# The last steps of a decode layer: inverse roots by one power instruction, the residual's product ahead, a store of two rows

## The chip, the cores and the metric

The kernel runs on one core of a Trainium2 chip. The metric is the device time of one execution in microseconds (us), and the number compared is the median of several runs.

## The reference

One token (one row of 512 numbers) passes two blocks:

```
h   = x + A(layernorm(x))
out = h + B(layernorm(h))

A: q = x @ wq                      (512 -> 32 heads of 128)
   8 key/value heads, 16384 cached positions, 4 query heads to each
   softmax(q . k / sqrt(128)) @ v, then @ wo   (4096 -> 512)
B: one position, so the four shifted quarters of its mixer are all zero:
   x1 = x;  B = x1 + gelu(layernorm(x1) @ w3) @ w4   (512 -> 1792 -> 512)
layernorm(x) = (x - mean) / sqrt(var + 1e-5)
```

Block B gets a normalised row and normalises it again, so two inverse roots of nearly the same variance are needed at the end: `1/sqrt(v + eps)` for the residual and one of `v (1 + eps) + eps^2` for what goes into GELU. The output is `hr + (hr - mean) * root + gelu(...) @ w4`, where `hr` is the row h.

## The kernel before, in words

The work is written out by hand. A small `Program` class collects instructions for each engine in the order in which they are written, and derives the semaphore waits from the tiles that each reads and writes; `_run` issues an engine's instructions one after another. Nothing reorders them. `dve(None)` and `pe(None)` mark a branch that is never taken otherwise; what is written behind the mark lies in another block of code.

The stages are these. (1) The row's statistics: `row_sums(0, ...)` and `variance(0)` give mean and variance on all 128 partitions, `seeds` and `inverse_root` the root, and line 577 the normalised row `xn`. GpSimd (POOL) clears `qb` and `pt` meanwhile. (2) The query: 32 products with wq (L586). (3) Four passes over pairs of key/value heads: keys are loaded in 4 MB halves, transposed by VectorE (L609), multiplied (L626), softmax (L636 to L651), values multiplied (L662), gathered. (4) The output product with wo (L728), `osum`, `row_sums(1, ...)`, `hc`, 16 products with w3 (L746). (5) The tail: roots, GELU in two halves (L758), each transposed to `hcol` (L762), 14 chunks `m` of 4 products each with w4 (L772), the copy `fin` (L777), the store (L778).

All large loads are issued on SP's queue (helper `load`, L433) in the order in which they are written: wq, keys and values, then wo, w3 and w4 in pieces. w4 comes in four pieces, `W4 = ((0, 5), (5, 10), (10, 13), (13, 14))`, and the products of chunk m wait for the piece that holds m.

The inverse root before is an integer seed and three Newton steps:

```
    by(lambda e: e.tensor_scalar(vh, v, -0.5, None, ALU.mult), ...)
    for k in range(3):
        by(lambda e: e.tensor_scalar(z, y, y, vh, ALU.mult, ALU.mult), ...)
        by(lambda e, dst=dst: (...)(dst, z, 1.5, y, ALU.add, ALU.mult), ...)
```

At the end VectorE works out the root for GELU and GpSimd the other one at the same time; GpSimd goes on with `xs` and `xsum` (L753, L755). `xsum`, the residual, is added by a product with the identity matrix into the accumulator of the w4 products (L768), behind chunk 9. The accumulator `n_ps` has 128 rows: the 32 rows of quarter o all hold the same 128 outputs, and the store takes one row of each quarter.

## Time and profile before

| | us |
|---|---|
| median of 3 runs | 191.78 |
| the runs | 191.37 to 191.93 |
| span of the profiled execution, first to last instruction | 190.4 |
| time of the profiled execution outside its span | not given |

| engine | busy us | share of the span |
|---|---|---|
| TensorE (PE) | 118.6 | 62% |
| VectorE (DVE) | 118.2 | 62% |
| ScalarE (ACT) | 9.3 | 5% |
| GpSimd (POOL) | 7.3 | 4% |

The DMA engines moved 79.20 MB at a mean of 416 GB/s. In the rows of the profile, a time in front is the start in us from the first instruction of the program, the next number is the length; x32 is a count; what stands behind <- in square brackets is what ended the engine's idle time before the row. A row of the windows has the stretch, its length, the busy time of each engine with its count, the granted TensorE clock (1.00 is full), the share of the DMA engines and GB/s.

### The profile page before, as it was taken

To read this page: it belongs to the slowest core of one execution; us is meant where nothing else is said; L and a number is where in the kernel's file an instruction comes from. 1 tells how busy PE (TensorE), PEld (TensorE's weight loads), DVE (VectorE), ACT (ScalarE), POOL (GpSimd) and SP (SyncE) were. 2 spreads that over 40 slices of the span, in tenths; PEclk is the share of its full clock that TensorE was granted. 3 is DMA by queue.
4 is the path that set the end of the run, shared out by engine and by line. 5 is a ranking of instruction groups with operands and counts; after the bars stand their busy time and mean duration, and the time that the engine had idled before them with its cause. 6 is when DMAs were issued, how large, how long until landed. Compare 5 with 4: busy or idle time off the path is not lost.

```text
span 190.4 us, 2182 instructions
## 1 busy us (share of the span) xinstructions
PE 118.6 (62%) x695; PEld 46.1 (24%) x695; DVE 118.2 (62%) x155; ACT 9.3 (5%) x16; POOL 7.3 (4%) x16
## 2 busy tenths in 40 slices
PE   0119709996195599940944989508449995294644
PEld 0103203442031143310311433203113332031212
DVE  6740799995504989845049989350479895504370
ACT  3000000000200000011000000020000000500020
POOL 7100000000000000000000000000000000000060
PEclk9999985899958579995585899975979999758855
DMA  6999999999999999997999999979999999989991
GB/s 227 434 441 441 441 441 441 441 441 441 413 441 406 420 523 441 441 441 330 441 441 441 523 441 413 441 324 420 413 441 441 441 441 441 441 367 421 409 411 51
DMA packets 3619, 79.20 MB, mean 416 GB/s; under 512 B 416, under 2 KB 544, under 8 KB 1568
## 3 DMA queue, kind: packets, MB, share of 16 engines
q1 hardware_dynamic: 3608, 79.17, 97.2%
q8 instruction: 1, 0.02, 0.0%
q14 instruction: 2, 0.02, 0.0%
q10 hardware_dynamic: 8, 0.00, 0.0%
HBM read 79.17 MB, written 0.00 MB: 416 GB/s over the span
## 4 chain that ended last, share of the span: by engine, by line
PE 39%; DMA 37%; DVE 16%; issue 4%; ACT 2%; ACTq 0%; SPq 0%; DVEq 0%
DMA kb<-in_A_k_cache_dram 31%; PE banks L626 22%; PE banks L662 6%; DMA vb<-in_A_wq_dram 6%; DVE kt L609 6%; PE banks L586 5%; DVE pt L651 3%; PE banks L728 2%; DVE mx L636 1%; ACT p_sb L647 1%; PE banks L620 1%; DVE od L681 1%; PE banks L772 1%; DVE qcol L593 1%; PE banks L639 1%
## 5 line engine op out<-in xcount | busy, mean ns | idle before, releaser
L609 DVE STREAM_TRANSPOSE kt<-kb 128x2048 int32<-128x2048 int32 (+1 forms) x37 | 71.3, 1987 | 4.3 <-DMA kb<-in_A_k_cache_dram 2.8
L626 PE MATMUL banks<-kt,qn 128*128 x256 | 68.7, 414 | 0.5
L626 PEld LDWEIGHTS banks<-kt,qn 128*128 x256 | 26.2, 102 | 41.4 <-issue 24.6
L662 PE MATMUL banks<-vb,pt 128*32 128x512 bf16 x256 | 24.4, 565 | 2.8 <-POOLq L448 2.8
L678 DVE TENSOR_SCALAR od<-banks,rowc 128x128 f32<-128x128 f32 x4 | 1.4, 350 | 26.3 <-PE banks L662 26.3
L620 PE MATMUL banks<-qn 128*128 128x512 bf16 x8 | 4.0, 495 | 17.3 <-DVE kt L609 17.1
L651 DVE STREAM_TRANSPOSE pt<-p_sb 64x1024 bf16<-64x1024 bf16 x8 | 9.9, 1239 | 5.4 <-ACT p_sb L647 5.3
L662 PEld LDWEIGHTS banks<-vb,pt 128*32 128x32 bf16 x256 | 9.0, 136 | 16.4 <-issue 12.4
L586 PE MATMUL banks<-vb,xn 128*128 x32 | 8.9, 446 | 6.1 <-DVE xn L577 6.1
L669 PE MATMUL banks<-acc,zd 128*32 128x1 f32 x8 | 1.1, 202 | 17.7 <-DVE pt L651 17.7
L647 ACT ACTIVATE p_sb<-banks,bias 128x1024 bf16<-128x1024 f32 x4 | 4.5, 1113 | 155.4 <-DVE nmh L643 155.4
L636 DVE TENSOR_REDUCE mx<-banks 128x1 f32<-128x1024 f32 x4 | 4.9, 1224 | 8.1 <-PE banks L626 8.1
L593 DVE STREAM_TRANSPOSE qcol<-banks 64x1024 f32<-64x1024 f32 x4 | 4.8, 1226 | 6.9 <-PE banks L586 6.9
L528 POOL TENSOR_SCALAR st<-st 128x1 f32<-128x1 f32 x1 | 0.2, 241 | 176.1 <-DVE st L513 176.1
L586 PEld LDWEIGHTS banks<-vb,xn 128*128 128x128 bf16 x32 | 3.6, 112 | 11.0 <-issue 8.5
L639 PE MATMUL banks<-mxd,mean 128*128 128x128 f32 x8 | 2.0, 326 | 6.6 <-DVE mxd L637 6.6
L620 PEld LDWEIGHTS banks<-qn 128*128 128x128 bf16 x8 | 0.8, 100 | 20.2 <-issue 20.0
L684 PE MATMUL banks<-od,zo 128*32 128x128 f32 x8 | 1.6, 285 | 6.5 <-DVE od L681 6.5
L669 PEld LDWEIGHTS banks<-acc,zd 128*32 128x32 f32 x8 | 0.7, 140 | 18.4 <-DVE pt L651 18.4
L681 DVE SCALAR_TENSOR_TENSOR od<-banks,rowc,od 128x128 f32<-128x128 f32 x12 | 4.2, 351 | 0.4
L550 DVE CAST ident<-ident_f 4x4 bf16<-4x4 f32 x1 | 3.8, 3848 | 0.6 <-POOL ident_f L545 0.6
L728 PE MATMUL banks<-kb,o_b 128*32 128x512 bf16 x32 | 3.5, 583 | 1.1 <-DVE o_b L724 1.1
(78 smaller groups left out, 44.6 us busy)
## 6 DMA issues: line engine op xcount, KB each, us to landing
kb<-in_A_k_cache_dram SPq DMA_DIRECT2D x8, 4096.0 KB, 29.7
vb<-in_A_v_cache_dram SPq DMA_DIRECT2D x2, 4096.0 KB, 29.2
vb<-in_A_wq_dram SPq DMA_DIRECT2D x1, 4096.0 KB, 12.3
kb<-in_A_wo_dram SPq DMA_DIRECT2D x2, 1536.0 KB, 25.4
kb<-in_B_w_dram SPq DMA_DIRECT2D x2, 640.0 KB, 25.4
kb<-in_B_w_dram SPq DMA_DIRECT2D x1, 896.0 KB, 22.4
kb<-in_B_w_dram SPq DMA_DIRECT2D x2, 448.0 KB, 23.4
kb<-in_A_wo_dram SPq DMA_DIRECT2D x1, 768.0 KB, 28.5
```

Source lines behind the costliest of these rows:

```text
L586: pe(lambda e, k=k: e.matmul(row[:, bass.ds(P.b, 512)], copies(xn[:, k:k + 1], 128), wq_k[:, k, bass.ds(P.c, REP * DH)], start=(k == 0), s ...
L593: dve(lambda e, g=g, b=b, half=half: e.transpose(qcol[64 * g:64 * g + 64, 2 * b:2 * b + 2, :, :].rearrange("p e m u -> p (e m u)"), half.r ...
L609: P.op("DVE", lambda e, view=view: e.transpose(view(kt), view(kb[y])), r=[("r", y, i) for i in range(RPARTS)], w=[("kt", t + i) for i in r ...
L620: pe(lambda e: e.matmul(row[:, bass.ds(P.y, 512)], copies(none, 128), copies(none, 512), start=True, stop=False, skip_group_check=True), r ...
L626: pe(lambda e, n=n: e.matmul(row[:, bass.ds(P.y, 512)], qn[:, n, bass.ds(P.q, 128)], key_piece(P.k, n), start=False, stop=(n == 3), skip_g ...
L636: dve(lambda e: e.tensor_reduce(mx[:, :], s_all, AX.X, ALU.max), r=[("s", 0), ("s", 1)], w=["mx"], **both)
L639: pe(lambda e: e.matmul(m_ps[:, 0:128], mean4[:, :], mxd[:, :], start=True, stop=True), r=["mxd", "mean4"], w=["m"], bank=["mn"])
L647: act(lambda e: e.activation(p_sb[:, :], s_all, ACTF.Exp, bias=bias[:, 0:1], scale=float(SCALE), accum_out=acc[:, :]), r=[("s", 0), ("s", ...
L651: dve(lambda e, g=g: e.transpose(pt[64 * g:64 * g + 64, :, :, g, :], p_sb[64 * g:64 * g + 64, :]), r=["p"], w=["pt"])
L662: pe(lambda e, l=l, ct=ct, ch=ch: e.matmul(O_ps[0][32 * ct:32 * ct + 32, :], pt[:, l, ch, :, :].rearrange("p g u -> p (g u)"), tiles[:, l ...
L681: dve(lambda e, block=block, c=c: e.scalar_tensor_tensor(od[:, :], block, rowc[:, c:c + 1], od[:, :], ALU.mult, ALU.add), r=[key, "rowc", ...
L728: pe(lambda e, r_=r_, q=q: e.matmul(O_ps[0][32 * q:32 * q + 32, :], copies(o_b[:, r_:r_ + 1], 32), wo_sb[:, r_ * D:(r_ + 1) * D], start=(r ...
```

## The change

Three things are done in the tail, and one in both places where a root is needed.

The roots: `seeds` and `inverse_root` go; a tile `expo` of two columns is filled with -0.5 by GpSimd, and one GpSimd `tensor_tensor` with the operation `pow` gives the root, of one column in the first layer norm and of two columns at once in the last. In the first, this instruction stands in GpSimd's order ahead of the two clearing instructions for `qb` and `pt`. `xs` and `xsum` are worked out by VectorE, ahead of the two transposes to `hcol`, and only the second needs the root.

The residual's product stands behind chunk 6 instead of chunk 9, and is made in four products of 32 columns.

The quarters of the accumulator are filled in the order 0, 2, 1, 3 (`BLOCK`). ScalarE copies the lower 64 rows to the left half of `fin`, VectorE the upper 64 rows to the right half, and the store takes rows 31 and 32 of `fin`, two rows of 256 numbers (512 bytes), where before it took four rows of 128 (256 bytes). VectorE's copy is behind the mark `dve(None)`.

```diff
+BLOCK = (0, 2, 1, 3)
...
-        def seeds(i, ns):
...
-        def inverse_root(i, n, by):
...
+            for n in range(1 + i):
                 mul, add = (1.0 + EPS, EPS * EPS) if n else (1.0, EPS)
                 dve(lambda e, n=n, mul=mul, add=add: e.tensor_scalar(s[:, 4 + n:5 + n], s[:, 3:4], mul, add,
                                                                      ALU.mult, ALU.add), r=[(S, 3)], w=[(S, 4 + n)])
...
+            pool(lambda e: e.tensor_tensor(s[:, 6:7 + i], s[:, 4:5 + i], expo[:, 0:1 + i], ALU.pow),
+                 r=["expo"] + [(S, 4 + n) for n in range(1 + i)], w=[(S, 6 + n) for n in range(1 + i)])
...
+        pool(lambda e: e.memset(expo[:, :], -0.5), w=["expo"])
...
         variance(0)
-        seeds(0, (0,))
-        inverse_root(0, 0, dve)
         act(lambda e: e.activation(scr[0:1, 0:1], mean4[0:1, 0:1], ACTF.Exp), r=["mean4"], w=["scr"])
         pool(lambda e: e.memset(qb[:, :, :, :], 0.0), w=["qb"])
         pool(lambda e: e.memset(pt[:, :, :, :, :], 0.0), w=["pt"])
...
         variance(1)
-        seeds(1, (0, 1))
-        inverse_root(1, 1, dve)
-        inverse_root(1, 0, pool)
-        pool(lambda e: e.tensor_scalar(xs[:, :], hr[:, :], s[:, 0:1], s[:, 6:7], ALU.add, ALU.mult),
-            r=["hr", (S, 0), (S, 6)], w=["xs"])
-        pool(lambda e: e.tensor_tensor(xsum[:, :], hr[:, :], xs[:, :], ALU.add), r=["hr", "xs"], w=["xsum"])
+        dve(lambda e: e.tensor_scalar(xs[:, :], hr[:, :], s[:, 0:1], None, ALU.add), r=["hr", (S, 0)], w=["xs"])
+        dve(lambda e: e.scalar_tensor_tensor(xsum[:, :], xs[:, :], s[:, 6:7], hr[:, :], ALU.mult, ALU.add),
+            r=["hr", "xs", (S, 6)], w=["xsum"])
...
         for m in range(NHC):
+            if m == NHC // 2:
+                for o in range(4):
+                    pe(lambda e, o=o: e.matmul(
+                        n_ps[32 * o:32 * o + 32, 0:128], ident_f[:, 32 * BLOCK[o]:32 * BLOCK[o] + 32], xsum[:, :],
+                        start=False, stop=False, skip_group_check=True),
+                       r=["ident_f", "xsum"], w=["n"], bank=["mn"])
             if m == W4[-2][0]:
-                pe(lambda e: e.matmul(n_ps[:, 0:128], ident_f[:, :], xsum[:, :], start=False, stop=False,
-                                      skip_group_check=True), r=["ident_f", "xsum"], w=["n"], bank=["mn"])
                 pe(None)
             for o in range(4):
                 pe(lambda e, m=m, o=o: e.matmul(
-                    n_ps[32 * o:32 * o + 32, 0:128], hcol[:, m, :], w4_sb[:, m, o * 128:(o + 1) * 128],
+                    n_ps[32 * o:32 * o + 32, 0:128], hcol[:, m, :], w4_sb[:, m, BLOCK[o] * 128:(BLOCK[o] + 1) * 128],
...
-        act(lambda e: e.activation(fin[:, :], n_ps[:, 0:128], ACTF.Identity), r=["n"], w=["fin"], bank=["mn"])
-        P.op("SP", lambda e: e.dma_start(out[0, 0:1, :].rearrange("o (q j) -> (o q) j", q=4), fin[0:128:32, :]),
-             r=["fin"], w=["out"], dma="out")
+        act(lambda e: e.activation(fin[:, 0:128], n_ps[0:64, 0:128], ACTF.Identity),
+            r=["n"], w=[("fin", 0)], bank=["mn"])
+        dve(lambda e: e.tensor_copy(fin[:, 128:256], n_ps[64:128, 0:128]), r=["n"], w=[("fin", 1)], bank=["mn"])
+        P.op("SP", lambda e: e.dma_start(out[0, 0:1, :].rearrange("o (q j) -> (o q) j", q=2), fin[31:33, :]),
+             r=[("fin", 0), ("fin", 1)], w=["out"], dma="out")
```

More of the change, by code (lines that the diff above doesn't have):

```diff
@@ L386, in bass_sequential_preLN__gqa_block_cached__mixer_s_mlp__decode_kernel @@
         st = [sb(f"st{i}", [128, 16], FP32) for i in range(2)]
-        sti = [sb(f"sti{i}", [128, 4], I32) for i in range(2)]
+        expo = sb("expo", [128, 2], FP32)
         xn = sb("xn", [128, NCH], BF16)
@@ L414, in bass_sequential_preLN__gqa_block_cached__mixer_s_mlp__decode_kernel @@
         hcol = sb("hcol", [128, NHC, 32], BF16)
-        fin = sb("fin", [128, 128], BF16)
+        fin = sb("fin", [64, 256], BF16)
         kb_all = sb("kb", [128, 256 * DH], BF16)
@@ L503, in variance @@
                 r=[(S, 2)], w=[(S, 3)])
-        def seeds(i, ns):
-            s, t = st[i], sti[i]
-            S, T = ("st", i), ("sti", i)
-            lo, hi = min(ns), max(ns) + 1
-            for n in ns:
+            for n in range(1 + i):
                 mul, add = (1.0 + EPS, EPS * EPS) if n else (1.0, EPS)
@@ L514, in seeds @@
                                                                      ALU.mult, ALU.add), r=[(S, 3)], w=[(S, 4 + n)])
-            dve(lambda e: e.tensor_single_scalar(t[:, 2 + lo:2 + hi], s[:, 4 + lo:4 + hi].bitcast(I32), 1,
-                                                 ALU.arith_shift_right),
-                r=[(S, 4 + n) for n in ns], w=[(T, 2)])
-            dve(lambda e: e.tensor_scalar(t[:, lo:hi], t[:, 2 + lo:2 + hi], -1, 1597463007,
-                                          ALU.mult, ALU.add), r=[(T, 2)], w=[(T, n) for n in ns])
-        def inverse_root(i, n, by):
-            s, t = st[i], sti[i]
-            S, T = ("st", i), ("sti", i)
-            v, y = s[:, 4 + n:5 + n], t[:, n:n + 1].bitcast(FP32)
-            z = s[:, 8 + n:9 + n]
-            vh = s[:, 10 + n:11 + n]
-            by(lambda e: e.tensor_scalar(vh, v, -0.5, None, ALU.mult), r=[(S, 4 + n)], w=[(S, 10 + n)])
-            for k in range(3):
-                dst, key = (s[:, 6 + n:7 + n], (S, 6 + n)) if k == 2 else (y, (T, n))
-                by(lambda e: e.tensor_scalar(z, y, y, vh, ALU.mult, ALU.mult),
-                   r=[(T, n), (S, 10 + n)], w=[(S, 8 + n)])
-                by(lambda e, dst=dst: (e.scalar_tensor_tensor if by is dve else e.tensor_scalar)(
-                    dst, z, 1.5, y, ALU.add, ALU.mult),
-                   r=[(S, 8 + n), (T, n)], w=[key])
+            pool(lambda e: e.tensor_tensor(s[:, 6:7 + i], s[:, 4:5 + i], expo[:, 0:1 + i], ALU.pow),
+                 r=["expo"] + [(S, 4 + n) for n in range(1 + i)], w=[(S, 6 + n) for n in range(1 + i)])
         load("x4", x4[:, :], A_x[0, 0:1, :].rearrange("o (q j) -> (o q) j", q=4), "x4", "ACT")
```

## The prediction

> **What bounds the kernel now.** I read the page first (its span and the 40 slices), then the chain that ended last, then the timeline of the last 12 us, and last the issue and landing of the last weight pieces.

> ```profile
> span 190.4 us, 2182 instructions
> DMA  6999999999999999997999999979999999989991
> GB/s 227 434 441 441 441 441 441 441 441 441 413 441 406 420 523 441 441 441 330 441 441 441 523 441 413 441 324 420 413 441 441 441 441 441 441 367 421 409 411 51
> ```

> A slice is 4.76 us. The 16 DMA engines are busy from the first slice to the last but one, near 441 GB/s: the kernel is the time to read its weights and caches, and after that a tail. What lies under the stream can be shortened without any effect on the end. So I need the moment at which the stream's last pieces land. The last three pieces of w4 are these, first their issue (start, length) and then their size and the time from issue to landing:

> ```profile
> 159.74 5.84 SPq L433 DMA_DIRECT2D kb<-in_B_w_dram  x1
> 165.63 3.16 SPq L433 DMA_DIRECT2D kb<-in_B_w_dram  x1
> 168.83 0.43 SPq L433 DMA_DIRECT2D kb<-in_B_w_dram  x1
> ...
> kb<-in_B_w_dram SPq DMA_DIRECT2D x1, 640.0 KB, 26.0
> kb<-in_B_w_dram SPq DMA_DIRECT2D x1, 384.0 KB, 21.1
> kb<-in_B_w_dram SPq DMA_DIRECT2D x1, 128.0 KB, 18.2
> ```

> Second piece (m = 5 to 9): 159.74 + 26.0 = 185.74. Third (m = 10 to 12): 165.63 + 21.1 = 186.73. Fourth (m = 13): 168.83 + 18.2 = 187.03. Against that stands the end of the chain:

> ```profile
> 80.21 29.02 DMA kb<-in_A_k_cache_dram
> ...
> 183.61 0.20 DVE st L533
> ...
> 183.89 0.49 ACT hg L758
> ...
> 184.41 0.59 DVE hcol L762
> ...
> 185.04 1.45 PE banks L772 x36
> 186.49 0.73 PE banks L768 x2
> 187.21 0.58 PE banks L772 x10
> ...
> 187.81 0.28 ACT fin L777
> ```

> The chain view draws a line from the root (L533) through GELU (L758), transpose (L762) and last product (L772) to the end. It hides that the weights were a second wait of nearly the same size:

> ```profile
> 185.76 0.46 PEld L772 LDWEIGHTS banks<-kb,hcol 128*32 128x32 bf16 x20 [0.26 <-DMA kb<-in_B_w_dram]
> 186.41 0.50 PEld L768 LDWEIGHTS banks<-xsum,ident_f 128*128 128x128 f32 x2 [0.20 <-issue]
> 187.14 0.62 PE L772 MATMUL banks<-kb,hcol 128*32 128x128 bf16 x16
> ```

> At 185.76, 0.02 after the second piece, TensorE resumed after a DMA wait. From there it never stopped until 187.76: twenty products, the residual's product (L768, 186.41 to 187.14), then the sixteen that need pieces three and four. When those sixteen began at 187.14, both pieces had landed, the last 0.11 before. So the residual's product, and not the stream, set the last 0.4 us of TensorE. Behind it stands a fixed tail: copy, store, landing.

> **The change part by part.** The sum is made on this profiled execution (span 190.4; its own time outside the span is not given), and the difference is put on the median of the runs, 191.78, which is 1.38 above the span.

> *Residual's product.* It becomes four products of 32 columns (8 passes in place of 2) behind m = 6 instead of m = 9. Since m = 5 and 6 need the second piece, it still runs after 185.74; it does not fall into the wait ahead of that. Its price at 32 columns is seen at one place, L734, the same shapes:

> ```profile
> 179.32 0.43 PE L734 MATMUL banks<-osum,row 128*32 128x128 f32 x8 [0.79 <-DVE osum L732]
> 179.30:179.47 0.17, 0.15 (x8) 0.16 (x8) 1.00 0.70 274
> 186.41:187.14 0.73, 0.73 (x6) 0.50 0.14 41
> ```

> L734 took 0.43 with its drain, but at a granted clock of 1.00 (the third number from the end); at 186.4 the clock is 0.50. A round of four L772 products costs 0.10: the sixteen took 0.62, which is three steps of 0.10 and 0.32 for the last round with its drain. The residual costs between 0.11 (0.43 less that drain, if the clock cost nothing) and 0.73 (as now); I take 0.5, nearest to the L734 row slowed by the clock. Then, from 185.76: two rounds, 185.96; residual, 186.46; three rounds for m = 7 to 9, 186.77; the third piece is there since 186.73, so three rounds, 187.08; the fourth piece since 187.03, last round 0.32, end at 187.40. Before, 187.76: **-0.36**. Bounds: with a residual of 0.11 the landing at 187.03 plus 0.04 plus 0.32 stops it at 187.39; with 0.73 it is 187.63, -0.13.

> *Both roots by one GpSimd instruction.* Gone are two DVE integer steps and seven DVE steps of the Newton root for GELU (181.80 to 183.81), and seven steps and two wide ones on GpSimd. Added: one power of 128x2 on GpSimd, and two 128x128 steps on DVE ahead of the transposes.

> ```profile
> 181.56 0.21 DVE L513 TENSOR_SCALAR st<-st 128x1 f32<-128x1 f32 x2
> 181.57 1.68 PE L746 MATMUL banks<-kb,hc 128*32 128x448 bf16 x16 [0.69 <-ACT hc L740]
> 181.80 0.24 POOL L528 TENSOR_SCALAR st<-st 128x1 f32<-128x1 f32 x1 [176.12 <-DVE st L513]
> 185.22 0.45 POOL L755 TENSOR_TENSOR xsum<-hr,xs 128x128 f32<-128x128 f32 x1
> ```

> The inputs are ready at 181.77, so the power starts about 181.83. No row shows a power. Its bounds are the GpSimd step of one element, 0.24, and the longest GpSimd span of the trace, 2.18 (L560, below); it is nearest to a TENSOR_TENSOR, 0.45, with more arithmetic, and I take 0.8. GELU could then start at 182.7, but the product L746 that it reads ends at 183.25: the wait moves there. GELU at 183.3 instead of 183.89, transposed 1.1 later, first L772 at about 184.45 instead of 185.04. Those 0.6 us end in the wait for the second piece at 185.74. So the power is worth **0**. It also costs 0 as long as the products behind it run unhindered to 187.40: seven rounds, 0.5, six rounds and 0.32 are 2.1, so they may start at 185.25, which puts the power's end at 184.0: up to 2.2 us it is free, and beyond that each us costs a us. The two DVE steps: each takes about 0.3 (the estimate for a 128-wide copy below); the first needs only the mean and runs under the power; the second waits for it, and the transposes are queued behind it, but these wait 0.49 for GELU anyway.

> *Start.* The first power stands in GpSimd's queue ahead of two memsets that before ran at once:

> ```profile
> 1.76 2.18 POOL L560 MEMSET qb<- 128x2496 bf16 x1
> 1.86 3.85 DVE L550 CAST ident<-ident_f 4x4 bf16<-4x4 f32 x1 [0.57 <-POOL ident_f L545]
> 3.88 1.80 POOL L561 MEMSET pt<- 128x2048 bf16 x1
> 8.29 0.15 DVE L513 TENSOR_SCALAR st<-st 128x1 f32<-128x1 f32 x1
> 13.00 0.29 DVE L577 TENSOR_SCALAR xn<-hT,st 128x4 bf16<-128x4 f32 x1 [1.35 <-DMA vb<-in_A_wq_dram]
> ```

> A cast of 4x4 took 3.85 us and ended as the memsets did: these two hold DVE up. With the memsets behind the power, DVE's chain starts up to 3.7 us earlier, and the memsets end between 9.5 and 13.2 (8.44 + 0.8 + 2.18 + 1.80, if nothing starts earlier). xn waits for wq until 13.00 in either case; at worst 0.2 is lost, under a stream whose engines don't go idle. Nine DVE steps fewer here: also **0**. Cover gone, the whole power would count once.

> *Copy of the result.* ScalarE copies 64 rows instead of 128, VectorE the rest, side by side.

> ```profile
> 178.57 0.69 DVE L732 COPY osum<-banks 128x512 f32<-128x512 f32 x1 [3.61 <-PE banks L728]
> 180.92 0.16 DVE L494 COPY st<-banks 128x2 f32<-128x2 f32 x1 [0.16 <-PE banks L492]
> ```

> The free size stays 128, so ScalarE's 0.28 stays. DVE's, between those two copies out of the same memory, is 0.16 + 0.53 x 126/510 = 0.29. SP now waits for two engines, one more queue step, like the 0.03 that now lies between the copy's end (187.81 + 0.28) and the store's issue at 188.12; behind it only the store is queued. Together **+0.04** (bounds 0, and +0.3 if the copies went one after the other).

> *Store of two rows of 512 bytes for four of 256.*

> ```profile
> 188.12 0.63 SPq L778 DMA_DIRECT2D out_dram<-fin  x1
> SPq L780 <- DMA out_dram<-fin: 1.6, 1, 1.6
> 189.30:189.50 0.20, 0.00 (x0) 0.00 (x0) 0.00 (x0) 0.00 (x0) 0.00 (x0) 0.50 0.03 5
> 189.50:190.30 0.80, 0.00 (x0) 0.00 (x0) 0.00 (x0) 0.00 (x0) 0.00 (x0) 0.50 0.00 0
> ```

> After the issue SP waits 1.6 us. The result's 1 KB moves between 189.3 and 189.5 (5 GB/s for 0.2 us); then nothing moves, and the last wait ends only at about 190.36 (188.12 + 0.63 + 1.6). In this silence of 0.87 SP waits for a write that has left already. It may stay whole (0, or +0.1 as each row is twice as long) or go (-0.87). With half as many, larger rows I take **-0.35**, somewhat under the middle. [...]

> Sum: -0.36 + 0 + 0 + 0.04 - 0.35 = -0.67, so 191.78 - 0.67 = **191.1 us**. The bounds add up to -1.3 (190.5) and +0.27 (192.0).

> **The rivals.** What a measurement of this kernel can tell from no change is about 0.3%, 0.58 us.

> *The store's silence stays.* Then only the product's 0.36 less 0.04 is won: 191.45, no measurable change. For it: nothing moves in the silence, so there is no size to save. Chance 0.23.

> *The silence goes.* If it is only there because the rows are small, -0.36 + 0.04 - 0.87 = -1.19, 190.6. Against it: a write of any size has some way to go. [...] Chance 0.10.

> *The stream takes it all.* The last pieces land so much later, or the residual costs its 0.73, that the product's gain shrinks to 0.1, and the store is as before: 191.7. Against it: the bytes and their queue don't change. Chance 0.05.

> *Slower: the power is long.* It replaces on the path what the roots took. It is free to 2.2 us, eats the gain at 2.9, and is measurably slower from 3.4 (2.2 + 0.67 + 0.58); at 4 us, 192.9. Against it: GpSimd's rows of this size take 0.24 to 0.45, so it would need eight times the longest. For it: none shows a power. Chance 0.09.

> *Slower: the power's code is cold.* GpSimd may have to fetch what it runs, on the second use again after 170 idle us. The nearest row of an engine that loads before it works is this:

> ```profile
> 1.30 1.28 ACT L559 ACT_TABLE_LOAD   x1 [1.30 <-PEq L797]
> ```

> With 1.28 ahead of 0.8 the power still ends inside its free 2.2; with twice that, 3.36, the time is 191.1 + 1.16 = 192.3, and from there on it is measurably slower. Against it: L528 ran in 0.24 after 176 idle us, and the first use, under the wq load, takes the first fetch. Chance 0.04. [...]

> *Slower: VectorE's half comes late.* It is the first VectorE instruction behind the branch at L150 and its block of code; if that block arrives only when asked for, SP waits for it, measurably so from 1.25 late (0.67 + 0.58): 192.4. Against it: the branch is passed behind the transposes, which move with GELU to about 184.9, 2.5 us ahead of the copy. Chance 0.06.

> **How the numbers follow.** The forecast has 0.43. With the silence gone, 0.10, nearly all of it is beyond 0.3% faster: 0.52. Within 0.3%: the store unchanged (0.23), the stream (0.05), the rest of the forecast and a little of the late half: 0.30. Slower: long power, cold code and most of the late half, 0.18. The range 190.5 to 192.0 takes in the forecast's bounds and the first three rivals, and leaves out the slow power, the cold code and the late half.

> **What would show it.** Right: GELU begins at the end of the w3 product near 183.3; the first L772 products stop for a DMA wait of about 0.8 ahead of 185.8; the last product ends 0.35 to 0.4 after the last piece lands; the two copies lie side by side; SP's last wait is about 1.25. Wrong: a power over 2.2 us, TensorE waiting on VectorE after 185.8, or SP's last wait still at 1.6.

## The result, and the profile after

The changed kernel takes 190.93 us (median of 5 runs, 190.71 to 191.29); the kernel before takes 191.78 beside it. The ratio on record is 0.9946, with a 95% interval from 0.9928 to 0.9964: faster by 0.4 to 0.7% (the quotient of the two medians alone is 0.9956). The forecast was 191.1 us, faster. The number was met; the mechanism behind most of it was not the one forecast, as the profile and then the experiments show.

The profiled execution took 191.29, the slowest of the five, with a span of 189.7. First the page of the changed kernel: its span, the engines with their busy time and their number of instructions, and the queues on which code is fetched (packets, MB, share).

```profile
span 189.7 us, 2177 instructions
PE 116.1 (61%) x701; PEld 45.8 (24%) x701; DVE 115.4 (61%) x140; ACT 9.3 (5%) x16; POOL 5.7 (3%) x10
q8 instruction: 1, 0.02, 0.0%
```

The same part of the page of before has 155 VectorE instructions instead of 140, and one queue more:

```profile
PE 118.6 (62%) x695; PEld 46.1 (24%) x695; DVE 118.2 (62%) x155; ACT 9.3 (5%) x16; POOL 7.3 (4%) x16
q8 instruction: 1, 0.02, 0.0%
q14 instruction: 2, 0.02, 0.0%
```

I had read over that line. The two fetches of code on q14 near the end of the kernel before are gone after the change; below this turns out to be most of the result.

Now the chain and the timeline of the tail after the change (start, length, what; in brackets the idle time and what ended it), with the issue of the last w4 piece and its time to landing in front:

```profile
160.12 25.99 DMA kb<-in_B_w_dram
169.22 0.43 SPq L434 DMA_DIRECT2D kb<-in_B_w_dram  x1
kb<-in_B_w_dram SPq DMA_DIRECT2D x1, 128.0 KB, 18.2
...
182.15 1.68 PE L720 MATMUL banks<-kb,hc 128*32 128x448 bf16 x16 [0.69 <-ACT hc L714]
182.44 0.70 POOL L509 TENSOR_TENSOR st<-st,expo 128x2 f32<-128x2 f32 x1 [173.01 <-DVE st L507]
183.89 0.85 ACT L729 ACTIVATE hg<-banks,st 128x224 bf16<-128x224 f32 x2 [1.79 <-PE banks L720]
186.16 0.41 PE L747 MATMUL banks<-kb,hcol 128*32 128x128 bf16 x8 [0.38 <-DMA kb<-in_B_w_dram]
186.34 0.65 PE L740 MATMUL banks<-xsum,ident_f 128*32 128x128 f32 x8
186.77 0.97 PE L747 MATMUL banks<-kb,hcol 128*32 128x128 bf16 x28
187.78 0.27 ACT L752 ACTIVATE fin<-banks 64x128 bf16<-64x128 f32 x1 [3.04 <-PE banks L747]
188.16 0.29 DVE L754 CAST fin<-banks 64x128 bf16<-64x128 f32 x1 [2.69 <-ACT fin L752]
188.52 0.33 SPq L755 DMA_DIRECT2D out_dram<-fin  x1
...
SPq L757 <- DMA out_dram<-fin: 0.8, 1, 0.8
```

- The power takes 0.70. GELU starts at 183.89 because the w3 product ended ("<-PE banks L720"), not because of the power. That is the same moment as before and not the forecast 183.3, since the w3 product itself began 0.58 later here (182.15 against 181.57).
- TensorE waits for the second w4 piece (it lands at 160.12 + 25.99 = 186.11). The last piece lands at 169.22 + 18.2 = 187.42, and the last product ends at 187.74, 0.32 later; before, it was 0.73 (187.76 against 187.03).
- The whole stream came 0.4 us later in this execution than in the profiled one of before (187.42 against 187.03), so ends are compared with the last landing: the span ends 2.3 us behind it, before 3.4 (190.4 against 187.03).
- The copies don't lie side by side. VectorE's began at 188.16 and what it waited for is "ACT fin L752", the other copy.
- The store is issued in 0.33 us instead of 0.63, and acknowledged in 0.8 instead of 1.6.

From the last landing: -0.4 by the product, +0.4 by the copies (last product to store 0.78 instead of 0.36), -1.1 by the store (issue 0.3, wait 0.8), together -1.1; the later stream took 0.4 of it back in this execution.

The start went as described: the power of one column took 0.56, the memsets held up a small VectorE copy instead of the cast, and xn waited for wq as before.

```profile
5.00 0.56 POOL L509 TENSOR_TENSOR st<-st,expo 128x1 f32<-128x1 f32 x1 [3.12 <-DVE st L507]
5.83 3.63 DVE L548 COPY zo<-rowgh 128x32 f32<-128x32 f32 x1
13.47 0.29 DVE L551 TENSOR_SCALAR xn<-hT,st 128x4 bf16<-128x4 f32 x1 [3.99 <-DMA vb<-in_A_wq_dram]
```

### The profile page after: what moved, and what is told of

Same layout as the page of the kernel before. It is cut to its first block, busy times and chain, and to the rows that moved or that the text cites. A ratio compares the mean times of both kernels' runs of the same rounds, so it can differ in the third digit from the quotient of the medians.

```text
span 189.7 us, 2177 instructions
## 1 busy us (share of the span) xinstructions
PE 116.1 (61%) x701; PEld 45.8 (24%) x701; DVE 115.4 (61%) x140; ACT 9.3 (5%) x16; POOL 5.7 (3%) x10
## 4 chain that ended last, share of the span: by engine, by line
DMA 66%; DVE 15%; PE 14%; issue 3%; SPq 1%; ACT 0%; DVEq 0%
DMA kb<-in_A_k_cache_dram 46%; DMA kb<-in_B_w_dram 14%; DVE kt L583 13%; PE banks L600 8%; DMA vb<-in_A_wq_dram 7%; PE banks L560 4%; SPq L434 1%; DVE qcol L567 1%; PE banks L594 1%; PE banks L747 1%; DVE qb L574 0%; PE banks L740 0%; DVE xn L551 0%; DVE fin L754 0%; ACT fin L752 0%
## 5 line engine op out<-in xcount | busy, mean ns | idle before, releaser
L600 PE MATMUL banks<-kt,qn 128*128 x256 | 69.8, 422 | 0.2
L636 PE MATMUL banks<-vb,pt 128*32 128x512 bf16 x256 | 22.8, 534 | 2.8 <-POOLq L449 2.8
L560 PE MATMUL banks<-vb,xn 128*128 x32 | 8.4, 428 | 10.1 <-DVE xn L551 10.1
L560 PEld LDWEIGHTS banks<-vb,xn 128*128 128x128 bf16 x32 | 3.5, 108 | 14.6 <-issue 11.8
L509 POOL TENSOR_TENSOR st<-st,expo 128x1 f32<-128x1 f32 (+1 forms) x2 | 1.3, 630 | 176.1 <-DVE st L507 176.1
L702 PE MATMUL banks<-kb,o_b 128*32 128x512 bf16 x32 | 2.7, 384 | 2.4 <-DMA kb<-in_A_wo_dram 1.3
L548 DVE COPY zo<-rowgh 128x32 f32<-128x32 f32 x1 | 3.6, 3627 | 0.0
```

What stands on the lines that cost most here:

```text
L548: dve(lambda e, z=z, m=m: e.tensor_copy(z[:, :].rearrange("p (n d) -> p n d", d=4), m[:, :, :].rearrange("p g h -> p (g h)").unsqueeze(2). ...
L560: pe(lambda e, k=k: e.matmul(row[:, bass.ds(P.b, 512)], copies(xn[:, k:k + 1], 128), wq_k[:, k, bass.ds(P.c, REP * DH)], start=(k == 0), s ...
L600: pe(lambda e, n=n: e.matmul(row[:, bass.ds(P.y, 512)], qn[:, n, bass.ds(P.q, 128)], key_piece(P.k, n), start=False, stop=(n == 3), skip_g ...
L636: pe(lambda e, l=l, ct=ct, ch=ch: e.matmul(O_ps[0][32 * ct:32 * ct + 32, :], pt[:, l, ch, :, :].rearrange("p g u -> p (g u)"), tiles[:, l ...
L702: pe(lambda e, r_=r_, q=q: e.matmul(O_ps[0][32 * q:32 * q + 32, :], copies(o_b[:, r_:r_ + 1], 32), wo_sb[:, r_ * D:(r_ + 1) * D], start=(r ...
```

## The experiments

After the result my theory was: the end is the last landing, and behind it come TensorE's rest, the copies and the store; the product and the store won, the power won nothing. The rival: the power shortened the path. The first four kernels take the parts one by one, and mend the copies.

**The copies side by side.** VectorE's copy waited because the program class orders two engines that name the same PSUM bank, even where both only read.

```diff
-        dve(lambda e: e.tensor_copy(fin[:, 128:256], n_ps[64:128, 0:128]), r=["n"], w=[("fin", 1)], bank=["mn"])
+        dve(lambda e: e.tensor_copy(fin[:, 128:256], n_ps[64:128, 0:128]), r=["n"], w=[("fin", 1)])
```

> The changed kernel, with VectorE's copy no longer made to wait for ScalarE's (both still wait for the last product). Theory: in the changed kernel the copies ran one after the other only because the program orders two engines at one PSUM bank; free of that they lie side by side, the store is issued 0.35 to 0.4 us after the last product ends instead of 0.76, and the time is 0.38 below the changed kernel's 190.93: about 190.55, 1.2 below the kernel before. Rival: two engines that read one bank at the same time slow each other down to the sum; then each copy takes up to 0.57 instead of 0.28 and less than 0.1 is won, about 190.9.

Measured: 190.58 against 192.02 before, ratio 0.9933 (0.992 to 0.9946). The timeline:

```profile
187.23 0.27 ACT L752 ACTIVATE fin<-banks 64x128 bf16<-64x128 f32 x1 [3.03 <-PE banks L747]
187.23 0.29 DVE L754 CAST fin<-banks 64x128 bf16<-64x128 f32 x1 [2.30 <-PE banks L747]
187.59 0.33 SPq L755 DMA_DIRECT2D out_dram<-fin  x1
```

Both copies start at once and neither gets longer. The store is issued 0.36 behind the copies' start instead of 0.74. The ratio alone, 0.13% below that of the changed kernel, doesn't settle the size; a second run below does.

**The store alone.** The kernel before with only the order of the quarters, the two copies and the store of two rows.

```diff
+        dve(lambda e: e.tensor_copy(ident_b[:, :].rearrange("p (b a u) -> p b a u", a=2, b=2),
+                                    ident_f[:, :].rearrange("p (a b u) -> p b a u", a=2, b=2)),
+            r=["ident_f"], w=["ident_b"])
...
-        act(lambda e: e.activation(fin[:, :], n_ps[:, 0:128], ACTF.Identity), r=["n"], w=["fin"], bank=["mn"])
+        act(lambda e: e.activation(fin[:, 0:128], n_ps[0:64, 0:128], ACTF.Identity), ...)
+        dve(lambda e: e.tensor_copy(fin[:, 128:256], n_ps[64:128, 0:128]), ...)
```

> The kernel before with only the order of the quarters, the two copies (one after the other, as in the changed kernel) and the store of two rows; roots and the residual's product as before (the product reads a permuted copy of the identity, made at the start). Theory: the store's issue goes from 0.63 to 0.33 and SP's last wait from 1.6 to 0.8, 1.1 together, and the second copy gives back 0.4: 0.7 below the kernel before, about 191.1. Rival: the short store of the changed kernel's profile is chance or hangs on the instructions that went from the roots; then the second copy alone remains, 0.4 above the kernel before, about 192.2.

Measured: 192.85 against 192.02, ratio 1.0049 (1.0035 to 1.0063): slower than either side expected (191.1 and 192.2), though the store was as short as the theory said. Its timeline, its wait, and the head of what the DMA view answers for the stretch from 189.5 to 190.1 and for the one from 190.2 to 193.0, behind the span:

```profile
188.56 0.29 DVE L784 CAST fin<-banks 64x128 bf16<-64x128 f32 x1 [2.54 <-ACT fin L782]
188.93 0.33 SPq L785 DMA_DIRECT2D out_dram<-fin  x1
SPq L787 <- DMA out_dram<-fin: 0.8, 1, 0.8
...
GB/s 0 0 0 0 0 0 0 0 0 0 0 0 68 0 1 0 0 0 0 0 0 0 546 0 0 0 0 0 0 0 0 0 0 0 0 0 0 0 0 0
q14 instruction: 1, 0.01, 4.9%
...
GB/s 0 0 0 0 0 0 0 0 0 0 0 0 0 0 0 0 0 0 0 0 0 0 0 0 0 0 0 0 0 0 0 0 0 0 117 0 0 0 0 0
q14 instruction: 1, 0.01, 0.7%
```

The strips have 40 slices, of 0.015 us in the first stretch and 0.07 in the second. The result's two rows move at 189.7, then 8 KB of code are fetched at 189.83, 1.0 us behind VectorE's last instruction (188.85), and again at 192.6, when the span (190.1) is long over. The execution took 193.13, 3.0 more than its span; the kernel before takes 1.4 more (192.30 for a span of 190.9 in one of its later runs). So code was still being loaded at the end, and the fetches moved with VectorE's last instruction, which is here the copy (the page counts 157 of them). In the kernel before, VectorE ends at 185.45, and the q14 fetches lie near 186.6 and 189.0, inside the span. That is the new theory (code): q14 is VectorE's; two fetches come behind its last instruction unless its program is short; the power made it short. What the fetched code is, no trace tells.

**The product alone.**

```diff
+            if m == NHC // 2:
+                for o in range(4):
+                    pe(lambda e, o=o: e.matmul(n_ps[32 * o:32 * o + 32, 0:128], ident_f[:, 32 * o:32 * o + 32], xsum[:, :], ...))
             if m == W4[-2][0]:
-                pe(lambda e: e.matmul(n_ps[:, 0:128], ident_f[:, :], xsum[:, :], ...))
                 pe(None)
```

> The kernel before with only the residual's product changed (four products of 32 columns behind chunk 6). Theory: TensorE is set by the landing of the last w4 pieces; the last product ends 0.37 after the last landing instead of 0.74, about 191.4, 0.36 below the kernel before. Rival: the path of the roots sets the end, and the product only moves within it: no change, 191.8.

Measured: 191.91 against 192.02, ratio 0.9995 (0.9979 to 1.001; 12 runs, from 190.75 to 192.40): no difference. But in the profiled execution not for the rival's reason. TensorE ended earlier, and that was lost in the store. First its timeline and waits, then the strip of the DMA view from 188.9 to 189.7, slices of 0.02 us; last, the strip of the kernel before from 188.9 to 189.5, slices of 0.015:

```profile
187.62 0.28 ACT L781 ACTIVATE fin<-banks 128x128 bf16<-128x128 f32 x1 [2.86 <-PE banks L776]
187.93 0.63 SPq L782 DMA_DIRECT2D out_dram<-fin  x1
SPq L784 <- DMA out_dram<-fin: 1.8, 1, 1.8
...
GB/s 0 0 0 0 0 0 0 0 410 0 0 0 13 13 13 0 0 0 0 0 0 0 0 0 0 0 0 0 0 0 0 0 0 13 0 0 0 0 0 0
q14 instruction: 1, 0.01, 3.9%
...
GB/s 0 0 0 0 0 0 0 546 0 0 0 0 0 0 0 0 0 0 0 0 0 0 0 0 0 0 0 0 0 17 17 17 0 0 17 0 0 0 0 0
q14 instruction: 1, 0.01, 3.4%
```

The store was issued 0.19 earlier than in the kernel before (187.93 against 188.12), and ended no earlier: SP waited 1.8 instead of 1.6. The code fetch begins at 189.06, three of the four rows leave between 189.14 and 189.20, and the fourth at 189.56. In the kernel before, the fetch begins at 189.0 and all four rows leave between 189.33 and 189.43. Which row SP waits for is told by the trace's records of the store's semaphore: here three rows are acknowledged by 189.54 and the fourth at 190.41, in the kernel before three by 189.73 and the fourth at 190.36. So with the fetch one row of four is acknowledged 0.6 to 0.9 behind the others; without it, in the next kernel, all four come within 0.07 (189.54 to 189.61). VectorE ends at 185.49 here and at 185.45 before, and the fetch stays in its place with it when the store comes forward. How the fetch holds up a row that has left, as in the kernel before, the traces don't show.

**The power alone** (roots by the power, xs and xsum on VectorE; product, copy and store as before).

> The kernel before with only the roots by one power (and xs, xsum on VectorE); product, copy and store as before. Theory: GELU starts at the end of the w3 product, up to 0.6 earlier, and TensorE then waits for the w4 piece that lands 1 us later: no change, 191.8 within 0.15. Rival: the root's chain, which the chain view shows on the path, is the bound: 0.5 to 0.6 less, about 191.2.

Measured: 191.15 against 192.02, ratio 0.9963 (0.995 to 0.9976). My theory, that the power is worth nothing, fell; but the rival's reason isn't what the trace shows either:

```profile
183.35 0.85 ACT L729 ACTIVATE hg<-banks,st 128x224 bf16<-128x224 f32 x2 [1.79 <-PE banks L720]
185.62 0.72 PE L743 MATMUL banks<-kb,hcol 128*32 128x128 bf16 x20 [0.38 <-DMA kb<-in_B_w_dram]
187.97 0.63 SPq L749 DMA_DIRECT2D out_dram<-fin  x1
SPq L751 <- DMA out_dram<-fin: 1.0, 1, 1.0
```

TensorE waits for w4 as forecast. What is shorter is SP's last wait: 1.0 for the same four rows of 256 bytes, and the page has no q14.

So the next runs set the length of VectorE's program by itself.

**The changed kernel with a longer VectorE program.**

```diff
+        for i in range(24):
+            dve(lambda e, i=i: e.memset(pad[:, i:i + 1], 0.0), w=[("pad", i)])
         dve(lambda e: e.tensor_scalar(xn[:, :], hT[:, :, 0], ...))
```

> The changed kernel with 24 one-element memsets more on VectorE, put into its idle time before the wq load has landed. They take nothing on the path. Theory (code): VectorE's program is then again longer than in the kernel before; about 1.0 us after its last instruction, the copy, its queue q14 fetches 8 KB of code, and again some 2.6 us later, as in the run of the store alone; the span stays at about 189.4, but the program ends 1.3 to 2 us later: 192.3 to 192.9. Rival: the length of VectorE's program is of no account, and the fetches in the other runs are a matter of chance: 190.9, as the changed kernel.

Measured: 193.20 against 191.99, ratio 1.0064 (1.0046 to 1.0083). 24 one-element memsets at the start turn the gain of 0.5% into a loss of 0.6%. The form differs from what I expected: the copy itself came late, so the span grew too (191.8).

```profile
187.20 0.27 ACT L755 ACTIVATE fin<-banks 64x128 bf16<-64x128 f32 x1 [2.46 <-PE banks L750]
190.23 0.29 DVE L757 CAST fin<-banks 64x128 bf16<-64x128 f32 x1 [4.78 <-issue]
190.60 0.33 SPq L758 DMA_DIRECT2D out_dram<-fin  x1
q14 instruction: 2, 0.02, 0.0%
```

ScalarE's half was ready at 187.47; VectorE's began at 190.23, and its idle time of 4.78 is put down to "issue": it waited for nothing that a semaphore tells of. The first fetch on q14 begins in that time, at 188.45. The prediction's rival "VectorE's half comes late" is this; the changed kernel, which differs by the 24 memsets alone, escapes it by its shorter program. The second fetch begins at 191.13, ahead of the store's two rows (191.37), and yet SP's last wait is 0.8: in this one execution two rows were not held up as one of four is.

**The kernel before with a shorter VectorE program, without the power.**

```diff
-        dve(lambda e: e.memset(mean4[:, :], -1.0 / (32 * D)), w=["mean4"])
-        dve(lambda e: e.memset(ident_f[:, :], 0.0), w=["ident_f"])
+        pool(...)  # both
...
-        dve(lambda e: e.tensor_copy(ident[:, :], ident_f[0:4, 0:4]), r=["ident_f"], w=["ident"])
-        dve(lambda e: e.tensor_copy(quarter[:, :, :], ...))
+        pool(...)  # both
...
-        inverse_root(0, 0, dve)
+        inverse_root(0, 0, pool)
```

> The kernel before with both roots by Newton steps, but eleven instructions of the start moved from VectorE to GpSimd (two memsets, two small copies, the seven steps of the first root), all ahead of the landing of wq. Theory (code): VectorE's program gets nearly as short as with the power; no fetch on q14 near the end; the store of four rows is acknowledged in 1.0 instead of 1.6 us, and the time is 0.6 below the kernel before, as with the power alone. Rival (path): what the power won is the shorter chain to GELU; since that is as before here, the time is as before, 191.8 to 192.0, with SP's last wait still at 1.6.

Measured: 191.28 against 191.99, ratio 0.9961 (0.9948 to 0.9974): the gain of the power alone, without a power. SP's last wait is 1.0 and the page has no q14, though in this execution the Newton chain was on the path (TensorE waits for the transposes only, and GELU starts at the root's end):

```profile
184.70 0.85 ACT L758 ACTIVATE hg<-banks,st 128x224 bf16<-128x224 f32 x2 [2.37 <-DVE st L533]
185.85 1.26 PE L772 MATMUL banks<-kb,hcol 128*32 128x128 bf16 x40 [1.79 <-DVE hcol L762]
SPq L780 <- DMA out_dram<-fin: 1.0, 1, 1.0
```

**The power alone, with VectorE's program as long as before**, the other way round (run last; 14 one-element memsets in the same place).

> The kernel before with only the roots by one power (and xs, xsum on VectorE), and 14 one-element memsets more in VectorE's idle time at the start, so that VectorE's program is as long as in the kernel before. Theory (code): what the power alone won came from the shorter program; two fetches on q14 are back, one of them beside the store, SP's last wait is 1.6 instead of 1.0, and the time is that of the kernel before, 191.8 to 192.0. Rival (path): the shorter chain to GELU won it, whatever the length of the program: 191.15, 0.37% below the kernel before.

Measured: 192.02 against 191.88, ratio 0.9998 (0.9988 to 1.0009): no difference. Two q14 fetches are back, and SP's last wait is 1.7:

```profile
SPq L754 <- DMA out_dram<-fin: 1.7, 1, 1.7
q14 instruction: 2, 0.02, 0.0%
```

Short program without the power -0.39%, power without the short program -0.02%, both -0.37%: it is the length of the program. All fourteen profiles agree: with 139 to 144 VectorE instructions on the page there is no q14, and with 153 to 164 there is. Where between 144 and 153 the change lies, and whether it is the count itself that decides, wasn't tried.

**The changed kernel with the old copy and store.** Its diff is that of the store, backwards.

> The changed kernel with the copy and the store of before (one copy by ScalarE, four rows of 256 bytes, quarters in order); power and residual's product as in the changed kernel. Theory: the store alone, free of the code fetch, is issued in 0.63 instead of 0.33 and acknowledged in 1.0 instead of 0.8, and the second copy's 0.4 goes: 0.1 above the changed kernel, 191.0, no difference that can be measured. Rival (small rows): the size of the rows sets SP's last wait; it is back at 1.6, and the time 0.6 above the changed kernel, 191.5.

Measured: 190.91 against 191.99, ratio 0.9946 (0.9932 to 0.996), the ratio of the changed kernel to the fourth place. SP's last wait is 1.0 and the issue 0.63:

```profile
187.58 0.63 SPq L753 DMA_DIRECT2D out_dram<-fin  x1
SPq L755 <- DMA out_dram<-fin: 1.0, 1, 1.0
```

So in the changed kernel the two rows win 0.5 (issue 0.3, wait 0.2), the copies one after the other cost 0.4, and the whole third part of the change is worth nothing that can be measured.

**Two rows in two pieces each.**

```diff
-        fin = sb("fin", [64, 256], BF16)
+        fin = sb("fin", [64, 2, 160], BF16)
...
-        ... out[0, 0:1, :].rearrange("o (q j) -> (o q) j", q=2), fin[31:33, :]
+        ... out[0, 0:1, :].rearrange("o (q a j) -> (o q) a j", q=2, a=2), fin[31:33, :, 0:128]
```

> The changed kernel with the copies side by side, and each of the store's two rows in two pieces of 256 bytes that lie apart in the source: two rows, but four pieces under 512 bytes. Theory: issue (0.33) and last wait (0.8) hang on the number of rows, that is of queues, and stay as with two whole rows, within 0.1. Rival (small rows): pieces under 512 bytes are slow whatever their number; the last wait is back at 1.0 or more.

Measured (one run): 191.42. The issue took 0.80 and the last wait 1.0:

```profile
188.17 0.80 SPq L755 DMA_DIRECT2D out_dram<-fin  x1
SPq L757 <- DMA out_dram<-fin: 1.0, 1, 1.0
```

The theory is wrong, and the wait is the rival's: with four pieces of 256 bytes it is 1.0 in two rows as in four, with two of 512 bytes 0.8. Whether the size of the pieces or their number makes this difference isn't shown, since no run has another size or number. And that is 0.2 of the 0.8 which the change won on this wait; the other 0.6 is what four rows lose beside a fetch (1.6 with it, 1.0 without).

**Four powers in a row**, copies side by side. The first three write unused columns.

> The changed kernel with the copies side by side, and three more powers of two columns (into unused columns) ahead of the one that is read, in the last layer norm. Theory: each takes about 0.6 to 0.7, together 2.4 to 2.8, so the last power ends some 2 us later; up to about 2.2 a power is free, so the last product ends 0.3 to 0.6 us later than with one power, 0.7 to 1.0 after the last w4 piece has landed instead of 0.36, and the time is 190.9 to 191.2. Rival (path): the power was on the path already; all of the added 1.8 to 2.1 us counts, about 192.5.

```profile
184.07 0.69 POOL L512 TENSOR_TENSOR st<-st,expo 128x2 f32<-128x2 f32 x1
187.16 0.97 PE L750 MATMUL banks<-kb,hcol 128*32 128x128 bf16 x28
168.87 0.43 SPq L434 DMA_DIRECT2D kb<-in_B_w_dram  x1
kb<-in_B_w_dram SPq DMA_DIRECT2D x1, 128.0 KB, 18.2
```

The last power ended at 184.76, where it would have ended at 182.8 alone: 2.0 later. The last product ended at 188.13, 1.06 behind the last landing (168.87 + 18.2 = 187.07), with one power 0.32: of 2.0 us, 0.74 reached TensorE's end. That is a little more than the 0.3 to 0.6 expected, and far from all of it. The time is nevertheless the rival's: 192.45 (one run), 2.75 more than the span of 189.7. The fetch on q8 begins at 189.7 in this run, when the store is over, where it began between 186.7 and 188.2 in the others. Whether the 1.2 us that remain come from it, wasn't tried.

**Copies side by side, on one chip with the changed kernel.**

> The changed kernel with the two copies side by side, a second time, now on one chip with the changed kernel. Theory: 0.36 us, 0.19%, below the changed kernel. Rival: what the store's earlier issue wins is lost again, as in the first run, where the ratio to the kernel before was only 0.13% lower than the changed kernel's: less than 0.1 us.

> The changed kernel itself, beside the one with its copies side by side. Both theories: 0.5 to 0.6% below the kernel before.

Measured: side by side 190.63 (190.44 to 190.72), the changed kernel 191.00 (190.76 to 191.22), the kernel before 192.04. The ratios are 0.9923 (0.9906 to 0.9941) and 0.9941 (0.9923 to 0.996). The slowest of the six runs side by side is below the fastest of the changed kernel: 0.37 us, as the theory said. This version, 0.7 to 0.8% below the kernel before, beats both.

## Why the prediction was right, and where only its sum was

*What bounds the kernel: right.* The stream sets the end, and a tail stands behind it. What was read too shortly is the tail: the prediction took the silence of 0.87 us behind the store for the store's own, and passed over the "q14 instruction: 2" of the page. By the store's semaphore, 0.63 of that silence is one row alone (three acknowledged by 189.73, the fourth at 190.36).

*Residual's product: right in its size.* -0.36 was forecast for TensorE's end, and against the last landing it is -0.4 (0.32 instead of 0.73); the product itself held up the next one by 0.43 (186.34 to 186.77), where 0.5 was taken. By itself it was worth nothing (0.9995), since the store behind it ran into the fetch. Beside the power the ratio goes from 0.9963 to 0.9946 with it, 0.3 us, though the intervals overlap. That this cover had to go first was not in the prediction.

*The power: 0 on the path, as forecast, and yet the largest part of the result.* The power took 0.70 (0.8 taken), GELU began at the end of the w3 product, TensorE waited for the second piece (0.38, where about 0.8 was forecast). The step that failed is "Nine DVE steps fewer here: also 0", and its counterpart at the tail: the steps were counted as time alone. In all, VectorE has 15 instructions fewer (155 to 140); that is worth 0 as time on the path and 0.7 us as code, since the shorter program ends without two fetches behind VectorE's last instruction. The 2x2 of the runs shows that (short program 0.9961, power with a long program 0.9998, both 0.9963, neither 1). The free 2.2 us of the power were rather less: with the last power ending 2.65 us after the first began, TensorE's end moved by 0.74, and not by 0.45; in that execution the powers began at 182.11 instead of 181.83 for the same landing, and that 0.28 comes off the slack. Nor is the slack of the one profile of before there in every execution: in those of the store alone and of the shortened kernel the Newton chain itself was on the path.

*The copies: the step that was wrong.* +0.04 was taken, with +0.3 as the bound "if the copies went one after the other"; they did, +0.4, beyond that bound. The order follows from the `bank` lists, which any two engines share: it could have been read in the waits of the built program.

*The store: right in direction, mis-sized and put down to the wrong thing.* -0.35 was taken between 0 and -0.87; it came to -1.1: 0.3 by the issue, which the sum had at 0, 0.2 by two pieces of 512 bytes for four of 256, 0.6 by the missing fetch. Four rows of 256 bytes win these 0.6 too when the fetch goes (1.0 instead of 1.6); that two rows would have escaped the fetch without the shorter program is possible (0.8 in the padded kernel) but stands on one execution. The rival "the silence goes" was closest for the wait alone (0.8 of 0.87), and its reason, the small rows, is good for 0.2 of that at most (1.0 with four pieces of 256 bytes, 0.8 with two of 512). The shortest of the waits shown here is 0.8: no store came without one.

*The rivals on the other side.* Neither a long nor a cold power came: 0.56 at the first use, 0.70 at the second, for two columns. VectorE's late half didn't come either, but the padded kernel shows how near it was.

So the forecast of -0.67 came near the measured -0.85 (about -1.0 by the ratio) because two errors lay against each other: the loss by the copies was taken 0.36 too small, the gain by the store 0.75 too small. That they cancelled by half was luck.

## What to carry to other kernels

Near a kernel's end, look at the instruction queues of the page too: here, with fetches of code behind VectorE's last instruction, a store of four rows was waited for 1.6 us instead of 1.0, a copy came 2.8 us late, or the program ended 3.0 us behind its span instead of 1.4, and 11 instructions moved from the start of VectorE's program to GpSimd's (155 to 144) were worth 0.7 us at the kernel's end, though they took nothing on the path. Compare ends with the last landing, not with the clock, where a stream bounds the kernel. Take each part of a combined change alone before crediting it: here the part meant for the path won by the length of its code, one part showed nothing by itself, and one made things worse alone.
